# A fused attention and two-mixture kernel: key buffer by expert, half of one expert's low parts on GpSimd, a new order

## The chip, the cores and the metric

The kernel runs on one core of one Trainium2 chip. The metric is the device time of one execution in microseconds (us). Three runs of the kernel before took 522.6, 523.45 and 535.63 us; their median, 523.45 us, is the time before.

## The reference, cut to what matters

Three stages follow one another, each on 4 batches of 576 tokens of width 512.

1. Windowed attention with 8 heads of 64: four heads see the last 32 positions, four see every fourth of the last 128.
2. A mixture of 4 attention experts. Each expert `e` has its own `q = x @ wq[e]`, `k = x @ wk[e]`, `v = x @ wv[e]` of width 64, a causal softmax over all 576 positions, and an output projection `wo[e]`. Each token adds up its two best experts with softmax weights.
3. A mixture of 8 feed-forward experts (512 to 1024 to 512, with a relu). One expert per token: its own best, or that of the token before it where a local gate says so. The result is scaled by a softmax probability.

## The kernel before, in words

Products are made in float16 with split operands: a value becomes a high part (`hi`, rounded) and a low part (`lo`, what rounding lost), and a product is the sum of high by high, high by low and low by high. The helper `split` (line 476 on) makes both parts: ScalarE (ACT) writes `hi` as a scaled copy, VectorE (DVE) writes `lo` with one scalar-tensor-tensor instruction. For a kind of split that `KN` lists, ACT writes a second, float32 scaled copy `f32t` (three buffers), and GpSimd (POOL) subtracts `hi` from it. Before the change only the kind "x2" goes that way.

Stages 1 and 2 and the first three blocks of stage 3 ("early slots", `eslot`, line 1358 on) form one part. Its instructions are recorded first, each with an estimated cost, its dependencies and a unit number; `Plan.order` (line 284 on) then schedules them in a list and issues them on five in-order queues: TensorE (PE), DVE, ACT, POOL and SyncE (SP), which starts the DMAs. The unit offsets `OFF` are the priorities: among the instructions that could start first on an engine, the unit with the lower offset goes first. There are 263 units (a projection half, an attention unit, a tile of the output projection, and so on).

Dependencies in the planner come from `region` and `hits`: an operand is a range of partitions and a range of bytes, from its first to its last. Two operands with the same two-row stride can be told apart inside those ranges; an operand of one run and one of two rows can't. Outside the planner, the framework that places the semaphores finds its own dependencies between the instructions.

For each batch `proj` (line 740 on) multiplies the tokens with the query and key weights in four groups `m` (queries of experts 0 and 1, keys of 0 and 1, queries of 2 and 3, keys of 2 and 3). Each group is split into a buffer `qkhl`, and DMAs carry it to the places where the attention reads it: four small ones per query group into `qs`, four per key group into `kk`, one for each expert and half of the partitions. `kk` holds, for each partition, four experts by high and low part by 576 positions. It has two buffers in turn: that of batches 0 and 2 lies in the large tile `share` (its DMAs read `share<-qkhl` in the trace), that of batches 1 and 3 is a tile of its own (`kk<-qkhl`). An attention unit (`at_a`, line 830 on) takes one tile of queries and one, two or four experts, and multiplies with the high and the low part of each expert's keys.

After the last batch's attention and routing come 19 slots (`slot`, line 1334 on) in a fixed order, each with the two products of one block of 128 tokens, while the next slot's weights are loaded and split. That part is not planned and not changed.

`w_split` (line 1266 on) splits the first expert's weights for the early slots: eight chunks of 128x1024, each in two halves of 512 columns, 16 splits of kind "w". In the slots after them both parts are made over whole chunks on ACT and DVE directly.

Of the kernel before, what the change touches and what calls it, by code (L numbers as in the profile page):

```python
# [11 lines left out]
F16 = mybir.dt.float16  # L12
I32 = mybir.dt.int32
AF = mybir.ActivationFunctionType
OP = mybir.AluOpType
# [9 lines left out]
E1 = 4  # L25
# [3 lines left out]
STATIC = 21  # L29
NEG = -float(2.0 ** 60)  # L30
XW = DM + 1
OFF = (-5462.82, 15301.63, 15749.23, 2741.58, 15715.62, 23895.09, 23839.59, -4159.48, -20321.99, 19270.96, 3973.86,
# [26 lines left out]
KN = {"x0": (0, 1), "qk": (0, 1), "v2": (0, 1), "x2": (1, 1), "yt": (0, 1), "w": (0, 1), "f32t": 3,  # L59
      "early": 3, "pfl": (100000,), "wn": 224, "xp": "XA", "warm": 80, "off": OFF,  # L60
      "xgb": 3, "x2b": 3, "hx": "X", "hy": "A", "h2": "X", "fc": (0, 4),
      "banks": {"S": 2, "T": 2, "A": 2, "X": 1, "Y": 1}, "share": 32740, "emax": 23840,
# [376 lines left out]
def tile_attention_moe_moe(ctx: ExitStack, tc, qd, kd, vw, wqk, wvg, wo, woT, wg9, w1, w2,  # L439
# [36 lines left out]
    def split(src, hi, lo, scale, kind=None):  # L476
        c = CNT[kind] = CNT.get(kind, -1) + 1
        num, den = KN.get(kind, (0, 1))
        A.activation(hi, src, AF.Copy, scale=float(scale))
        if c % den >= num:  # L480
            V.scalar_tensor_tensor(lo, src, float(scale), hi, op0=OP.mult, op1=OP.subtract)
            return
        if not isinstance(src, View):
            P.scalar_tensor_tensor(lo, src, float(scale), hi, op0=OP.mult, op1=OP.subtract)
            return
        n = int(np.prod(hi.shape[1:]))
        f = sm.tile([128, 512], F32, name="f32t", bufs=KN["f32t"])
        r = src.shape[0]
        f = f[:r, :n] if len(hi.shape) < 3 else f[:r, :n].rearrange("p (a b) -> p a b", a=hi.shape[1])
        A.activation(f, src, AF.Copy, scale=float(scale))  # L490
        P.tensor_tensor(lo, f, hi, op=OP.subtract)
# [248 lines left out]
    def proj(b):  # L740
        xh, xl = XH[b], XL[b]
        qs = pr.tile([128, E1, S], F16, name="qs2")
        kk = pr.tile([128, 2, E1, S], F16, name="kk2")
        vh = pr.tile([128, NT, E1, 65], F16, name="vh2")
        vl = pr.tile([128, NT, E1, 65], F16, name="vl2")
        QK[b] = (qs, kk, vh, vl)
        for m in (0, 2, 1, 3):
            q = pr.tile([128, 2, S], F16, name="qkhl")
            for i in range(2):
                c = slice(288 * i, 288 * i + 288)  # L750
                o = ps("A", [128, 288])
                for d in range(4):
                    w = wh[:, d, m * 128:m * 128 + 128]
                    T.matmul(o, w, xh[:, d, c], start=(d == 0), stop=False)
                    T.matmul(o, w, xl[:, d, c], start=False, stop=False)
                    w = wl[:, d, m * 128:m * 128 + 128]
                    T.matmul(o, w, xh[:, d, c], start=False, stop=(d == 3))
                split(o, q[:, 0, c], q[:, 1, c], 2.0 ** -9, "qk")
                yield 1.45
            for par in range(2):  # L760
                r = slice(64 * par, 64 * par + 64)
                e = 2 * (m % 2) + par
                for z in range(2):
                    zr = slice(64 * z, 64 * z + 64)
                    if m < 2:
                        SQ.dma_start(qs[zr, e, :], q[r, z, :])
                    else:
                        SQ.dma_start(kk[zr, :, e, :], q[r, :, :])
        if b < 2:
            P.memset(vh[:, :, :, 64:65], 512.0)  # L770
            P.memset(vl[:, :, :, 64:65], 0.0)
# [58 lines left out]
    def at_a(u):  # L830
        b, t, es = UNITS[u]
        qs, kk, _, _ = QK[b]
        s = sm.tile([128, S], F32, name="s2")
        mx = tiny.tile([128, 4], F32, name="mx2")
        if t < 4:
            ext = 128 * t + 128
            p = ps("S", [128, len(es), ext])
            for z, e in enumerate(es):
                w = qs[:, e, 128 * t:128 * t + 128]
                T.matmul(p[:, z, :], w, kk[:, 0, e, :ext], start=True, stop=False)  # L840
                T.matmul(p[:, z, :], w, kk[:, 1, e, :ext], start=False, stop=True)
            for z, e in enumerate(es):
                V.tensor_tensor_reduce(out=s[:, ext * z:ext * z + ext], in0=p[:, z, :],
                                       in1=tri[:, 512 - 128 * t:640],
                                       scale=-esc, scalar=3.0e38, op0=OP.add, op1=OP.min,
                                       accum_out=mx[:, z:z + 1])
            for z, e in enumerate(es):
                c = slice(ext * z, ext * z + ext)
                A.activation(s[:, c], s[:, c], AF.Exp, scale=-1.0, bias=mx[:, z:z + 1])
        else:  # L850
            for z in range(2):
                p = ps("S", [128, 288])
                c = slice(288 * z, 288 * z + 288)
                for h, e in enumerate(es):
                    w = qs[:, e, 512:576]
                    o = p[64 * h:64 * h + 64, :]
                    T.matmul(o, w, kk[:, 0, e, c], start=True, stop=False)
                    T.matmul(o, w, kk[:, 1, e, c], start=False, stop=True)
                V.tensor_tensor_reduce(out=s[:, c], in0=p, in1=tri2 if z else tri[:, 0:288],
                                       scale=-esc, scalar=3.0e38, op0=OP.add, op1=OP.min,  # L860
                                       accum_out=mx[:, z:z + 1])
            V.tensor_tensor(mx[:, 2:3], mx[:, 0:1], mx[:, 1:2], op=OP.min)
            A.activation(s, s, AF.Exp, scale=-1.0, bias=mx[:, 2:3])
        UA[u] = s
# [660 lines left out]
```

## Time and profile before

| what | us |
|---|---|
| median of the runs shown | 523.45 |
| the runs | 522.6, 523.45, 535.63 |
| the profiled execution | 531.6 |
| its span, first to last instruction | 529.6 |
| around the span | 2.0 |
| planned part, to the first matmul of the 19 slots | 310.2 |
| 19 slots and the end | 219.4 |

Read it as two parts. In the planned part PE, DVE and ACT share the work in an order that the planner chose; in the 19 slots PE works without a pause. The clock that the chip grants TensorE is one of two levels, 2.4 and 1.2 GHz; the profile writes them as 1.00 and 0.50, and its mean over the span is 0.964.

### The profile page before, as it was taken

The numbers are of one execution on the slowest core, as the hardware profiler recorded it, in microseconds if no ns is written. First come the engines' busy times: TensorE is split into PE (matmuls) and PEld (weight loads), VectorE is DVE, ScalarE is ACT, GpSimd is POOL, SyncE is SP. The second block draws the span as 40 slices with busy tenths as digits, with TensorE's granted clock in tenths as the row PEclk, the third lists the DMA queues.
The fourth block names the chain that finished last, engine by engine and source line by source line (L and its number), as shares of the span: only waits on it lengthen the run. The fifth ranks groups of instructions, "written<-read, shape, count | busy, mean of one in ns | idle before, by whom it ended". The sixth has DMA issues, their size and how long they took to land.

```text
span 529.6 us, 17318 instructions
## 1 busy us (share of the span) xinstructions
PE 499.1 (94%) x6802; PEld 384.5 (73%) x6802; DVE 423.3 (80%) x1225; ACT 370.3 (70%) x624; POOL 136.4 (26%) x165
## 2 busy tenths in 40 slices
PE   7799789999999999999799999999999999999992
PEld 6688678888887787776566776777767776677760
DVE  4855467788669879899897249999999999999993
ACT  4353344565666757687484159999999999999992
POOL 7845315341000001132200212132111321123211
PEclk9959978999999999999889999999999999999997
DMA  9773866332422321122571753774146199461110
GB/s 317 308 242 110 262 195 223 114 109 59 98 55 47 76 48 43 44 81 71 175 295 33 238 200 117 274 256 155 45 168 231 35 336 399 167 226 58 61 45 15
DMA packets 32727, 79.90 MB, mean 151 GB/s; under 512 B 7166, under 2 KB 15870, under 8 KB 31616
## 3 DMA queue, kind: packets, MB, share of 16 engines
q1 hardware_dynamic: 28960, 67.71, 37.8%
q0 software_dynamic: 3680, 11.03, 6.1%
q8 instruction: 55, 0.90, 0.7%
q14 instruction: 32, 0.26, 0.2%
HBM read 112.52 MB, written 10.49 MB: 232 GB/s over the span
## 4 chain that ended last, share of the span: by engine, by line
PE 40%; issue 23%; DMA 22%; DVE 9%; ACT 2%; POOL 1%; POOLq 0%; SPq 0%; DVEq 0%; ACTq 0%
DMA out_dram<-o,SIDX 17%; PE A L416 17%; PE S L416 6%; PE T L416 6%; PE X L416 6%; PE Y L416 4%; DVE s L416 2%; DVE tl L416 2%; DMA share<-in_vw_dram 2%; DMA share<-x2d,GIDX 1%; DMA share<-qkhl 1%; DVE share L416 1%; DVE r L416 1%; ACT share L1273 1%; DVE OHV L416 1%
## 5 line engine op out<-in xcount | busy, mean ns | idle before, releaser
L1274 DVE SCALAR_TENSOR_TENSOR share<-share 128x1024 f16<-128x1024 f32 x152 | 177.4, 1219 | 16.5 <-ACT share L1273 16.5
L1273 ACT ACTIVATE share<-share 128x1024 f16<-128x1024 f32 x152 | 149.9, 1048 | 0.6 <-DMA share<-in_w_dram 0.5
L416 PEld LDWEIGHTS <-share 128*128 128x128 f16 (+1 forms) x1438 | 112.4, 101 | 45.4 <-issue 7.3
L1308 PE MATMUL S<-share 128*128 128x128 f16 x608 | 102.8, 219 | 0.0
L1307 PE MATMUL S<-share 128*128 128x128 f16 x608 | 102.8, 219 | 0.0
L1309 PE MATMUL S<-share 128*128 128x128 f16 x608 | 102.8, 219 | 0.0
L416 PE MATMUL A<-share 128*128 128x288 f16 (+3 forms) x816 | 88.9, 267 | 3.9 <-DVE qkhl L416 3.7
L1328 POOL DMA_INDIRECT out_dram<-o,SIDX x19 | 27.0, 1418 | 155.0 <-ACT o L1325 146.9
L1308 PEld LDWEIGHTS <-share 128*128 128x128 f16 x608 | 59.5, 98 | 2.3
L1307 PEld LDWEIGHTS <-share 128*128 128x128 f16 x608 | 59.5, 98 | 2.3
L1309 PEld LDWEIGHTS <-share 128*128 128x128 f16 x608 | 59.5, 98 | 0.0
L1319 PE MATMUL A<-share 128*128 128x512 f16 x152 | 57.7, 380 | 0.0
L1321 PE MATMUL A<-share 128*128 128x512 f16 x152 | 57.4, 378 | 0.0
L1320 PE MATMUL A<-share 128*128 128x512 f16 x152 | 57.4, 378 | 0.0
L416 ACT ACTIVATE th<-T 128x512 f16<-128x512 f32 (+3 forms) x84 | 42.1, 513 | 21.3 <-PE T L416 20.1
L416 ACT ACTIVATE s<-s,mx 128x512 f32<-128x512 f32 (+4 forms) x72 | 40.7, 582 | 14.6 <-DVE mx L416 13.2
L416 ACT ACTIVATE share<-A 128x288 f16<-128x288 f32 (+3 forms) x67 | 30.0, 447 | 27.2 <-PE A L416 22.0
L416 POOL TENSOR_TENSOR share<-f32t,share 128x512 f16<-128x512 f32 (+1 forms) x15 | 16.0, 1067 | 117.8 <-ACT f32t L416 71.9
L416 DVE CUSTOM_DVE_ANT_0 s<-S,tri 128x256 f32<-128x256 f32 (+4 forms) x80 | 37.1, 476 | 9.1 <-PE S L416 8.7
L416 PE MATMUL S<-share 128*64 128x64 f32 (+5 forms) x672 | 38.7, 252 | 2.0 <-DMA share<-qkhl 2.0
L416 DVE SCALAR_TENSOR_TENSOR tl<-T,th 128x512 f16<-128x512 f32 (+2 forms) x60 | 35.6, 595 | 1.0 <-ACT th L416 0.8
L416 PE MATMUL T<-ident,s 128*128 128x128 f32 (+1 forms) x200 | 33.1, 285 | 0.8 <-ACT s L416 0.7
(207 smaller groups left out, 940.2 us busy)
## 6 DMA issues: line engine op xcount, KB each, us to landing
share<-in_w_dram SPq DMA_DIRECT2D x160, 512.0 KB
share<-in_vw_dram SPq DMA_DIRECT2D x8, 1152.0 KB
share<-in_kd_dram SPq DMA_DIRECT2D x8, 608.0 KB
share<-in_qd_dram SPq DMA_DIRECT2D x8, 576.0 KB
x2d<-share SPq DMA_DIRECT2D x16, 256.0 KB
share<-qkhl SPq DMA_DIRECT2D x16, 144.0 KB
kk<-qkhl SPq DMA_DIRECT2D x16, 144.0 KB
share<-share SPq DMA_DIRECT2D x16, 72.0 KB
```

The source lines that it names most:

```text
L416: getattr(q, name)(*[bind(x) for x in a], **{n: bind(x) for n, x in k.items()})
L1273: A.activation(h, stg[:, c, :], AF.Copy, scale=64.0)
L1274: V.scalar_tensor_tensor(l, stg[:, c, :], 64.0, h, op0=OP.mult, op1=OP.subtract)
L1307: T.matmul(p[:, i, :], wh_[:, c], xt[:, d, :], start=(d == 0), stop=False)
L1308: T.matmul(p[:, i, :], wh_[:, c], xt[:, 4 + d, :], start=False, stop=False)
L1309: T.matmul(p[:, i, :], wl_[:, c], xt[:, d, :], start=False, stop=(d == 3))
L1319: T.matmul(p, hh[:, f, :], wh_[:, a], start=(f == 0), stop=False)
L1320: T.matmul(p, hh[:, f, :], wl_[:, a], start=False, stop=False)
L1321: T.matmul(p, hl[:, f, :], wh_[:, a], start=False, stop=(f == 7))
L1328: return nc.gpsimd.indirect_dma_start(out=orows, out_offset=bass.IndirectOffsetOnAxis(ap=SIDX[:, t:t + 1], axis=0), in_=o, in_offset=None, ...
```

## The change

Three things. The key buffer becomes four experts by two parts by 576 positions, instead of two parts by four experts by 576, so that one expert's high and low rows lie next to each other, and each DMA fills one run per partition. The kind "w" gets the setting (1, 2): every second half-chunk split of the first expert's weights takes the `f32t` and POOL way. And all unit offsets are new numbers. A branch of `split` in which POOL would read a source from SBUF directly, and which no kind reached before, is gone.

```diff
 OFF = (...264 numbers, all replaced...)
-KN = {"x0": (0, 1), "qk": (0, 1), "v2": (0, 1), "x2": (1, 1), "yt": (0, 1), "w": (0, 1), "f32t": 3,
+KN = {"x0": (0, 1), "qk": (0, 1), "v2": (0, 1), "x2": (1, 1), "yt": (0, 1), "w": (1, 2), "f32t": 3,
@@ split
         if c % den >= num:
             V.scalar_tensor_tensor(lo, src, float(scale), hi, op0=OP.mult, op1=OP.subtract)
             return
-        if not isinstance(src, View):
-            P.scalar_tensor_tensor(lo, src, float(scale), hi, op0=OP.mult, op1=OP.subtract)
-            return
@@ proj
-        kk = pr.tile([128, 2, E1, S], F16, name="kk2")
+        kk = pr.tile([128, E1, 2, S], F16, name="kk2")
@@
-                        SQ.dma_start(kk[zr, :, e, :], q[r, :, :])
+                        SQ.dma_start(kk[zr, e], q[r, :, :])
@@ at_a
-                T.matmul(p[:, z, :], w, kk[:, 0, e, :ext], start=True, stop=False)
-                T.matmul(p[:, z, :], w, kk[:, 1, e, :ext], start=False, stop=True)
+                T.matmul(p[:, z, :], w, kk[:, e, 0, :ext], start=True, stop=False)
+                T.matmul(p[:, z, :], w, kk[:, e, 1, :ext], start=False, stop=True)
@@
-                    T.matmul(o, w, kk[:, 0, e, c], start=True, stop=False)
-                    T.matmul(o, w, kk[:, 1, e, c], start=False, stop=True)
+                    T.matmul(o, w, kk[:, e, 0, c], start=True, stop=False)
+                    T.matmul(o, w, kk[:, e, 1, c], start=False, stop=True)
```

## Rows read from the trace of the kernel before

**Rows 1.** The page's first part: busy time, share of the span, instructions.

```profile
PE 499.1 (94%) x6802; PEld 384.5 (73%) x6802; DVE 423.3 (80%) x1225; ACT 370.3 (70%) x624; POOL 136.4 (26%) x165
```

**Rows 2.** Busy time by stretch: start:end, length, each engine's busy us, granted clock, DMA share.

```profile
26.00:42.00 16.00, 15.42 (x286) 12.82 (x286) 7.96 (x39) 7.04 (x17) 8.98 (x18) 0.57 0.70 243
...
70.00:80.00 10.00, 8.50 (x131) 7.86 (x131) 6.02 (x32) 4.42 (x12) 2.28 (x2) 0.66 0.75 244
80.00:86.00 6.00, 6.00 (x146) 5.48 (x146) 4.37 (x37) 2.96 (x6) 4.32 (x3) 0.72 0.70 255
86.00:250.00 164.00, 162.33 (x2427) 129.22 (x2425) 134.73 (x571) 108.68 (x253) 31.55 (x23) 1.00 0.27 76
250.00:266.00 16.00, 11.81 (x155) 9.51 (x151) 12.88 (x72) 6.99 (x15) 4.30 (x4) 0.89 0.53 179
266.00:282.00 16.00, 16.00 (x155) 10.27 (x155) 15.95 (x38) 12.64 (x24) 0.00 (x0) 0.89 0.56 214
...
310.00:520.00 210.00, 209.34 (x2434) 154.34 (x2432) 197.87 (x190) 197.82 (x229) 48.22 (x38) 1.00 0.47 165
```

**Rows 3.** Timeline of PE and ACT: start, length, instruction, idle time before and releaser.

```profile
56.87 0.42 ACT L416 ACTIVATE share<-share 128x264 f16<-128x264 f32 x1 [2.51 <-DMA share<-in_wvg_dram]
...
60.06 0.88 PE L416 MATMUL A<-share 128*64 128x132 f16 x24 [3.73 <-DVE qkhl L416]
...
69.21 0.27 PE L416 MATMUL S<-share 128*128 128x256 f16 x1
71.50 1.28 PE L416 MATMUL S<-share 128*128 128x256 f16 x11 [2.02 <-DMA share<-qkhl]
```

**Rows 4.** The same timeline for SP's queue, around the key DMAs.

```profile
48.96 5.44 SPq L416 DMA_DIRECT2D share<-qkhl  x4
54.49 0.54 SPq L416 DMA_DIRECT2D share<-in_wvg_dram  x1
...
61.14 8.27 SPq L416 DMA_DIRECT2D share<-qkhl  x4
...
121.00 2.59 SPq L416 DMA_DIRECT2D kk<-qkhl  x4
```

**Rows 5.** Waits of SP's queue: for what, us in total, times, longest.

```profile
SPq L416 <- DMA share<-qkhl: 9.6, 6, 2.8
...
SPq L416 <- DMA share<-in_vw_dram: 2.4, 1, 2.4
```

**Rows 6.** Stretches of 2 us around the two pauses, columns as in rows 2.

```profile
58.00:60.00 2.00, 0.00 (x0) 0.00 (x0) 0.45 (x2) 1.23 (x3) 0.00 (x0) 1.00 1.03 373
...
70.00:72.00 2.00, 0.50 (x6) 0.48 (x7) 0.26 (x1) 0.17 (x1) 0.00 (x0) 0.99 0.85 216
72.00:74.00 2.00, 2.00 (x56) 1.80 (x57) 1.61 (x12) 1.35 (x4) 0.00 (x0) 0.50 1.04 401
```

**Rows 7.** Issues of the key and query DMAs: shortest, median, longest in ns.

```profile
L416 SPq DMA_DIRECT2D qs<-share x16: 462/575/1567, 95.8 to 218.6; - x16
...
L416 SPq DMA_DIRECT2D kk<-qkhl x16: 591/608/697, 121.0 to 192.0; - x16
```

**Rows 8.** Groups by shape: two of 263 to 283 us, two of the span.

```profile
L416 DVE SCALAR_TENSOR_TENSOR share<-share 128x512 f16<-128x512 f32 x16 | 10.4, 672 | 0.2 <-issue 0.2
L416 ACT ACTIVATE share<-share 128x512 f16<-128x512 f32 x16 | 9.0, 623 | 0.0
...
L416 POOL TENSOR_TENSOR share<-f32t,share 128x512 f16<-128x512 f32 x12 | 14.0, 1166 | 110.4 <-ACT f32t L416 64.7 <-PE A L416 31.5 <-ACT th L416 6.7
L416 ACT ACTIVATE f32t<-A 128x512 f32<-128x512 f32 x12 | 7.1, 591 | 0.0
```

**Rows 9.** Timeline of POOL and DVE where they overlap.

```profile
30.72 0.82 POOL L416 TENSOR_TENSOR share<-share,r 128x378 f32<-128x378 f32 x1 [0.94 <-DVE r L416]
31.33 0.75 DVE L416 SCALAR_TENSOR_TENSOR share<-share 128x512 f16<-128x512 f32 x1 [0.39 <-ACT share L416]
31.50 1.27 POOL L416 TENSOR_TENSOR share<-share,mx 128x378 f32<-128x378 f32 x1
```

More of the change, by code (lines that the diff above doesn't have):

```diff
@@ L31 @@
 XW = DM + 1
-OFF = (-5462.82, 15301.63, 15749.23, 2741.58, 15715.62, 23895.09, 23839.59, -4159.48, -20321.99, 19270.96, 3973.86,
[26 rows of a table removed]
-KN = {"x0": (0, 1), "qk": (0, 1), "v2": (0, 1), "x2": (1, 1), "yt": (0, 1), "w": (0, 1), "f32t": 3,
+OFF = (15079.06, -14073.05, -6228.6, -13230.76, -11311.75, -9136.75, -14304.07, 29513.66, -6714.41, -9107.27,
[26 rows of a table added]
+KN = {"x0": (0, 1), "qk": (0, 1), "v2": (0, 1), "x2": (1, 1), "yt": (0, 1), "w": (1, 2), "f32t": 3,
       "early": 3, "pfl": (100000,), "wn": 224, "xp": "XA", "warm": 80, "off": OFF,
```

52 rows, old and new, of the table OFF are left out of this document.

## The prediction, made before the change was run

> **What bounds the kernel now.** I read the page's busy shares first, then busy time by stretch, then the waits of the stretches with pauses. PE is busy 94% of the span [rows 1], so a saving is a pause of PE that closes or a stretch in which its clock rises again. By stretch [rows 2] most of the span has neither: from 86 to 250 us PE is busy 162.33 of 164 us, and in the slots, 310 to 520, 209.34 of 210, all at the full clock. The change doesn't touch the slots. What is left stands in three places. From 26 to 42 us the clock is at 0.57: (1 - 0.57) x 16 = 6.9 us are lost there. From 56 to 86 us PE pauses twice, for 3.73 and 2.02 us [rows 3], and the clock then falls: 0.66 over 10 us and 0.72 over 6 us lose 3.4 + 1.7 = 5.1 us [rows 2]. From 250 to 266 us PE idles 16 - 11.81 = 4.2 us, and the clock's 0.89 there and in the next 16 us loses 2 x 1.8 = 3.5 us.
>
> Both pauses of the second place lead back to the key DMAs. In SP's queue the four for batch 0's first key group take 5.44 us and those for the second 8.27 us, against 2.59 us for four of batch 1, whose buffer is a tile of its own [rows 4]. The difference is waiting: SP waited six times, 9.6 us in all, for an earlier `share<-qkhl` [rows 5]. Nothing in the data asks for that, since the four fill different places. But a two-row write of one expert spans, from its first byte to its last, the rows of the others, and a wait of up to 2.8 us between such writes is what a dependency on overlapping ranges looks like. What stands behind it in SP's queue pays: the load of a slice of `wvg` is issued at 54.49 us, right after the four [rows 4]; ACT, in order, sits 2.51 us until it lands, the eviction of `qkhl` behind it is late, and PE pauses 3.73 us for it [rows 3]. The second group's last DMA is late in the same way, and PE, one matmul into its first attention unit, pauses 2.02 us for it [rows 3].
>
> **The change part by part.** *Key layout.* Each write becomes one run per partition, disjoint from every other, so the waits between them should go, in the planner's dependencies too: a unit of experts 0 and 1 no longer needs the keys of 2 and 3. First term: the 2.8 us that SP is held before the `wvg` load [rows 5]. Of PE's 3.73 us this can return 0 (another load is the late one) to 3.7; I take the 2.51 us that ACT waited for exactly that load, 2.5. Next late would be the `wo` and `vw` loads in the same stretch. Second term: PE's pause for the second group, 0 to 2.0 us; I take 2.0, since units of experts 0 and 1 can fill it even if the DMAs stay late (SP's 2.4 us for `in_vw` [rows 5] is a load's and may stay). Third term: the clock. It was at 1.00 after PE had done nothing from 58 to 60 us, and at 0.50 from 72 us on, after a stretch in which PE was busy 0.50 of 2 us [rows 6]. If the pauses go, 0 to 5.1 us come back; the first pause left the clock up, the second didn't, so I take half, 2.5. The number of DMAs stays at 32, at 0.608 us each to issue; one run instead of two rows might bring them to the 0.575 us of a query write [rows 7], 32 x 0.033 = 1.1 us of SP, which has gaps: nothing.
>
> *Low parts on POOL.* Eight of the 16 half-chunks leave DVE: 8 x 10.4 / 16 = 5.2 us less there. ACT gets eight more copies, at 7.1 / 12 = 0.59 us [rows 8]: 4.7 us more. POOL gets 8 x 1.17 = 9.3 us and does nothing from 266 to 282 us [rows 2]. PE is busy 16.00 of 16 us in that stretch, so less DVE work there returns nothing at once: 0. The cover is PE's own backlog of output projection and early slots. If it is gone, ACT is the one to fear: 12.64 + 4.7 = 17.3 us of work in 16, 1.3 us too much. Everything behind those copies on ACT (evictions that free PSUM for PE) would wait as long. At best relieving DVE shortens the pauses just before, which belong to the last attention units, not to the weights; I bound the term at a gain of 1 and a loss of 4.1 us (the loss below) and take 0, since nothing in the rows shows PE short of work there.
>
> A POOL subtraction of 0.82 us took 1.27 us at 31.50 us, while DVE ran a split with two SBUF inputs [rows 9]: the two engines took turns. If that holds for the weights, eight POOL subtractions and the eight DVE splits left need 9.3 + 5.2 = 14.5 us in turn, where 16 splits on DVE needed 10.4: 4.1 us later, and only just inside the 16 us of the stretch. The Trainium skill, "SBUF — State Buffer", section "Who interferes with whom", has this as a rule: a DVE instruction with two SBUF inputs contends with a GpSimd instruction that reads SBUF, and whoever comes first keeps the port for the whole instruction. By the rule the sum would lose up to 4.1 us, by a POOL that is simply idle nothing; the trace agrees with the rule in the row at 31.50 us.
>
> *New order.* Every unit of the planned part moves, every queue is passed, and no instruction is added. From 86 to 250 us PE has 1.7 us of pauses to give [rows 2], so nothing there can gain. The gain is bounded by the third place, 4.2 + 3.5 = 7.7 us; the loss by a new low-clock stretch (below), 10.6. Neither is in the rows, so I take 0, between the two and nearest to 86 to 250 us, most of the part.
>
> *Sum.* 2.5 + 2.0 + 2.5 + 0 + 0 = 7.0 us, between 0 and 10.8 for the layout alone. Against the profiled execution, 531.6 us: 524.6. That one was 8.15 us above the median; none of my terms uses the stretch from 26 to 42 us, whose 6.9 us are the likeliest cause, so I take the 7.0 from the median: 523.45 - 7.0 = 516.5 us.
>
> **The rivals.** *The order pays too.* The layout's 7.0 us, and the new offsets put output projection into the pauses from 250 to 266 us: 6.5 of the 7.7 us. 510 us. For it: 4.2 us of pause with DVE busy 12.88 of 16 us [rows 2], and the low parts' move relieves DVE right behind. Against it: those units are the end of a chain that must run in sequence.
>
> *The port.* POOL and DVE take turns and the low parts come 4.1 us later: 516.5 + 4.1 = 520.6 us. For it [rows 9]; against it, the second product of the first early slot is what needs the last ones, and other PE work can go ahead.
>
> *The pauses only change their name.* DMA engines are busy all of 58 to 60 us, 1.03 [rows 6]; if the loads are what is late, PE waits for them instead, and the time stays at 523.5 us.
>
> *Slower: attention too early.* Units of experts 0 and 1 may now start around 56 us, in the place of projections. They are chains of PE, DVE, ACT and PE, with little PE work each; if PE becomes as thin as from 70 to 72 us [rows 6], the clock stays low for a stretch like 26 to 42 us, 6.9 us, with a pause like the 3.73 us: 10.6 more, 534 us. It decides once a pause like that of 70 to 72 us turns up early in the part with a 0.50 behind it.
>
> **How the numbers follow.** Chances: the forecast 0.40 (its own range 512 to 521 us), the order pays too 0.30, the port 0.10, the pauses stay 0.12, slower 0.08. The range 507 to 524 us leaves out the slower rival, and some of the order's best and the layout's worst, under 0.2 together. Two per cent, about what a measurement of this kernel can tell from no change, are 10.5 us: faster below 513.0, slower above 533.9. Faster: 0.8 of the order's 0.30 and 0.15 of the forecast's 0.40, 0.30. Slower: most of the last rival, 0.07. Within: 0.63.
>
> **What would show it.** SP's waits for `share<-qkhl` gone, and the four key DMAs of batches 0 and 2 in some 2.6 us as in batch 1; the first attention matmuls before the second key group has landed; no pause of PE over 1 us between 56 and 72 us, and the clock at 1.00 from 70 to 86; POOL subtractions of 1.17 us or more in the weights' stretch, DVE below 15.95 there; the first of the 19 slots some 7 us earlier, and their length unchanged. I am wrong if SP still waits between key writes, if loads hold PE from 56 to 60 us, or if the clock falls in a place where it was at 1.00.

## The result, and the profile after

The changed kernel took 520.04 us (median of 11 runs, 518.06 to 522.0), the kernel before, on the same chip, 525.84 us (11 runs, 522.6 to 535.63). The ratio is 0.9872, 95% interval [0.9839, 0.9905]: some 1.3% faster, within the 2%. On another chip a second set of runs gave 518.52 us and 0.984 [0.9763, 0.9916]. The forecast was 516.5 / 523.45 = 0.9867. Ratios and intervals leave out a kernel's runs that are over 1.5% above its fastest.

The profiled execution took 520.04 us, its span 518.2. The first slot's first matmul comes at 298.7 us (310.2 before), and slots and end last 219.5 us (219.4 before), so the 11.5 us between the two profiles lie wholly in the planned part. That pair shows more than the medians, since the execution profiled before was one of its longer ones. The page's first part, for [rows 1]:

```profile
PE 490.8 (95%) x6802; PEld 377.2 (73%) x6802; DVE 423.6 (82%) x1217; ACT 373.1 (72%) x632; POOL 145.8 (28%) x173
```

Eight instructions left DVE, and eight each came to ACT and POOL, as the weights' setting asks. Busy time by stretch of the changed kernel, for [rows 2] (start:end, length, busy us of PE, weight load, DVE, ACT, POOL, granted clock, DMA share, GB/s):

```profile
26.00:42.00 16.00, 13.25 (x249) 10.42 (x249) 9.14 (x48) 7.29 (x18) 10.22 (x19) 0.89 0.72 251
42.00:56.00 14.00, 13.40 (x288) 11.27 (x287) 10.53 (x59) 8.03 (x20) 8.92 (x15) 1.00 0.82 265
56.00:60.00 4.00, 4.00 (x87) 3.37 (x83) 3.06 (x28) 1.16 (x4) 0.63 (x1) 1.00 0.62 155
60.00:70.00 10.00, 9.19 (x198) 8.21 (x197) 7.71 (x35) 7.27 (x20) 5.73 (x4) 1.00 0.80 241
70.00:80.00 10.00, 10.00 (x169) 8.25 (x170) 8.22 (x53) 5.22 (x12) 5.45 (x4) 1.00 0.84 298
80.00:86.00 6.00, 6.00 (x106) 5.61 (x105) 4.63 (x26) 3.20 (x10) 4.32 (x3) 1.00 0.42 96
86.00:250.00 164.00, 159.46 (x2380) 125.91 (x2379) 137.28 (x590) 108.43 (x252) 25.55 (x21) 1.00 0.26 74
250.00:266.00 16.00, 13.11 (x133) 9.41 (x132) 10.20 (x24) 11.64 (x25) 8.45 (x8) 0.81 0.70 270
266.00:282.00 16.00, 16.00 (x216) 11.87 (x214) 14.16 (x54) 8.25 (x15) 4.32 (x4) 1.00 0.20 61
282.00:310.00 28.00, 28.00 (x299) 19.38 (x297) 11.88 (x16) 13.68 (x18) 5.43 (x5) 1.00 0.56 198
```

From 56 to 86 us PE idles 0.8 us of 30 at the full clock; before, its two pauses of 3.73 and 2.02 us and a clock of 0.66 and 0.72 stood there [rows 2, 3]. That place alone is worth some 10 us. From 26 to 42 us the clock is at 0.89 instead of 0.57, 5.1 us, while PE idles 2.2 us more: 3 us that no term of the prediction has. From 86 to 250 us PE idles 164 - 159.46 = 4.5 us, 2.8 more than before. From 250 to 266 us it idles 2.9 us instead of 4.2, and the clock is at 0.81 there instead of 0.89, and at 1.00 instead of 0.89 in the 16 us after it.

SP's queue and PE of the changed kernel by time, for [rows 4]:

```profile
43.34 3.51 SPq L416 DMA_DIRECT2D share<-qkhl  x4
48.06 0.38 SPq L416 DMA_DIRECT2D share<-in_wvg_dram  x1
54.44 1.75 SPq L416 DMA_DIRECT2D share<-qkhl  x3
60.09 0.51 SPq L416 DMA_DIRECT2D share<-qkhl  x1
```

```profile
49.87 0.60 PE L416 MATMUL S<-share 128*128 128x256 f16 x4
```

The first key group takes 3.51 us instead of 5.44. The second is sent in two pieces of 1.75 and 0.51 us, between 54.44 and 60.60 us, with other DMAs between them, where before it took 8.27 us in one go. The four matmuls at 49.87 us are attention of experts 0 and 1: they start before the second key group is sent at 54.44 us, as the disjoint ranges allow. What SP and PE waited for (us in all, times, longest; the first row is SP's only wait that has to do with `qkhl`, the other three are all of PE's between 26 and 75 us):

```profile
SPq L416 <- DVE qkhl L416: 16.0, 5, 4.9
```

```profile
PE S L416 <- POOL share L416: 1.9, 4, 0.8
PE T L416 <- POOL share L416: 1.6, 1, 1.6
PE X L416 <- DVE share L416: 0.3, 1, 0.3
```

SP's six waits for an earlier `share<-qkhl`, 9.6 us, and that for `in_vw` [rows 5] are gone. What is left is a wait for data: DVE has still to make the keys' low part. Before, that wait was 6.6 us, so in all SP waits as long for the keys as it did (16.0 against 9.6 + 6.6 us), but no longer for another key write.

### The profile page after: what moved, and what is told of

It is laid out like the page before. It is cut to its first block, busy times and chain, and to the rows that moved or that the text cites. A ratio compares the mean times of both kernels' runs of the same rounds, so it can differ in the third digit from the quotient of the medians.

```text
span 518.2 us, 17329 instructions
## 1 busy us (share of the span) xinstructions
PE 490.8 (95%) x6802; PEld 377.2 (73%) x6802; DVE 423.6 (82%) x1217; ACT 373.1 (72%) x632; POOL 145.8 (28%) x173
## 4 chain that ended last, share of the span: by engine, by line
PE 35%; issue 24%; DMA 23%; DVE 10%; POOL 3%; ACT 2%; POOLq 0%; SPq 0%; DVEq 0%; ACTq 0%
DMA out_dram<-o,SIDX 18%; PE A L416 17%; PE T L416 5%; PE S L416 5%; PE Y L416 4%; PE X L416 4%; DVE share L416 3%; POOL share L416 3%; DMA out_dram<-share,SIDX 2%; DMA share<-in_wo_dram 2%; DVE tl L416 1%; DVE s L416 1%; DVE r L416 1%; ACT share L416 1%; DMA share<-in_qd_dram 1%
## 5 line engine op out<-in xcount | busy, mean ns | idle before, releaser
L416 PE MATMUL A<-share 128*128 128x288 f16 (+3 forms) x816 | 87.6, 266 | 0.4 <-ACT L L416 0.2
L416 POOL TENSOR_TENSOR share<-f32t,share 128x512 f16<-128x512 f32 (+1 forms) x23 | 25.9, 1130 | 104.9 <-ACT f32t L416 92.3
L416 ACT ACTIVATE s<-s,mx 128x512 f32<-128x512 f32 (+4 forms) x72 | 40.5, 582 | 13.2 <-DVE mx L416 11.5
L416 PE MATMUL S<-share 128*64 128x64 f32 (+4 forms) x672 | 36.5, 236 | 2.5 <-POOL share L416 1.9
L416 DVE SCALAR_TENSOR_TENSOR share<-A,share 128x288 f16<-128x288 f32 (+3 forms) x52 | 24.2, 465 | 11.9 <-ACT share L416 11.6
```

Source lines behind the costliest of these rows:

```text
L416: getattr(q, name)(*[bind(x) for x in a], **{n: bind(x) for n, x in k.items()})
```

## The experiments

All kernels by what they contain; "old*" and "new*" mean that the planner was told the addresses of the other layout, so that every engine's order is that of the kernel which the row is compared with. Ratios are against the kernel before on the same chip.

| kernel | key layout | low parts on POOL | offsets | extra matmuls | ratio, 95% interval |
|---|---|---|---|---|---|
| changed kernel | new | half | new | no | 0.9872 [0.9839, 0.9905] |
| changed kernel, again | new | half | new | no | 0.984 [0.9763, 0.9916] |
| layout alone, order kept | new* | none | old | no | 0.9996 [0.994, 1.0052] |
| layout alone, planned anew | new | none | old | no | 0.9913 [0.985, 0.9976] |
| changed, old layout | old* | half | new | no | 0.9947 [0.9892, 1.0003] |
| changed, low parts on DVE | new | none | new | no | 0.9925 [0.9873, 0.9978] |
| low parts alone | old | half | old | no | 1.0058 [1.0022, 1.0094] |
| offsets alone | old | none | new | no | 1.0348 [1.0281, 1.0416] |
| changed, old offsets | new | half | old | no | 1.0017 [0.9966, 1.0068] |
| before, filled | old | none | old | 64 | 1.0012 [0.997, 1.0054] |
| layout alone, filled | new* | none | old | 64 | 0.9897 [0.9832, 0.9962] |
| changed, old layout, filled | old* | half | new | 64 | 0.9985 [0.9946, 1.0024] |
| changed, filled | new | half | new | 64 | 0.9887 [0.9825, 0.9949] |

**The layout alone, in before's order.** The instructions of every engine and their order are those of the kernel before; only the shape of the key DMAs and the addresses differ. The two lines that matter of the edit (the reads in `at_a` change too, and a function tells the planner the old addresses):

```diff
-        kk = pr.tile([128, 2, E1, S], F16, name="kk2")
+        kk = pr.tile([128, E1, 2, S], F16, name="kk2")
...
-                        SQ.dma_start(kk[zr, :, e, :], q[r, :, :])
+                        SQ.dma_start(kk[zr, e], q[r, :, :])
```

> The kernel before with the new key layout alone; every engine's instructions stay in the order of the kernel before. The waits theory (SP was held 9.6 us by waits between key writes, and that made the two pauses of PE at 56 and 69.5 us): SP's waits for share<-qkhl at 0, the pause of 3.73 us down to about 1.2, that of 2.02 us gone, 4 to 7 us less, a ratio of 0.987 to 0.992. The order theory (the gain comes from the new offsets): the waits may go, but loads end the pauses, ratio 0.998 to 1.002.

Measured: 0.9996 [0.994, 1.0052], the medians 528.42 and 530.2 us. The profile says more than that. Its stretches:

```profile
56.00:60.00 4.00, 3.34 (x65) 3.03 (x64) 3.04 (x17) 1.52 (x6) 2.34 (x3) 1.00 1.00 349
60.00:70.00 10.00, 9.06 (x193) 7.65 (x193) 6.66 (x47) 5.53 (x17) 1.62 (x2) 1.00 0.94 280
70.00:80.00 10.00, 9.53 (x183) 8.84 (x179) 8.13 (x56) 5.13 (x13) 6.60 (x5) 0.83 0.74 236
80.00:86.00 6.00, 5.96 (x85) 4.83 (x84) 5.10 (x28) 2.87 (x10) 3.32 (x2) 1.00 0.72 219
```

By time, its SP queue, ACT behind the `wvg` load, and PE:

```profile
48.79 2.38 SPq L416 DMA_DIRECT2D share<-qkhl  x4
57.91 4.96 SPq L416 DMA_DIRECT2D share<-qkhl  x4
...
54.72 0.42 ACT L416 ACTIVATE share<-share 128x264 f16<-128x264 f32 x1 [0.53 <-DMA share<-in_wvg_dram]
56.83 0.88 PE L416 MATMUL A<-share 128*64 128x132 f16 x24 [0.66 <-DVE qkhl L416]
66.39 0.38 PE L416 MATMUL S<-share 128*128 128x256 f16 x2 [0.24 <-DMA share<-qkhl]
67.46 0.82 PE L416 MATMUL S<-share 128*128 128x256 f16 x10 [0.70 <-DMA share<-in_kd_dram]
71.62 1.85 PE L416 MATMUL A<-wg,share 128*128 128x9 f32 x16
```

ACT's wait for the `wvg` load fell from 2.51 to 0.53 us, PE's pause behind it from 3.73 to 0.66, and the second from 2.02 to 0.24, with 0.70 us for another load behind it. From 56 to 86 us this leaves 2.1 us idle and 10 x 0.17 = 1.7 us of clock, 3.8 in all, where before had 5.75 + 5.1 = 10.85: 7.0 us back. The matmul on `wg`, which reads only what comes before, moved from 78.83 us to 71.62, and the slots start at 304.0 instead of 310.2. The second key group still takes 4.96 us, 2.5 of them SP's wait for the `in_vw` load. So the mechanism is there, and is worth 6 to 7 us in one pair of profiles, while the runs show nothing. The pair flatters it: the execution profiled here, 525.52 us, is the lowest of its six, that of before one of the longer. In the first set of runs that was the riddle.

**The layout alone, planned anew.** Here the planner sees the new layout's dependencies, with the old offsets and no low parts on POOL.

> The kernel before with the new key layout, and the planner sees it, so that it may start units of experts 0 and 1 earlier; offsets and the weights' low parts as before. The waits theory: as the run with the order kept, 4 to 7 us less, 0.987 to 0.992, and another 1 us at most from units that start earlier. The order theory: a plan with offsets that were not made for these dependencies is no better than before, 0.998 to 1.01.

Measured: 0.9913 [0.985, 0.9976]. But the order is hardly another one: by operation, shape and tile, 8 of 1225 places in DVE's order, 4 of 624 in ACT's and 16 of 6802 in PE's hold another instruction than before, and none in POOL's and SP's. So this is nearly the same program as the one above, and yet the counted runs of the two, on one chip, differ by 4.4 +- 2.7 us. Taken together they are 2.2 +- 2.8 us faster than before: from these two alone the layout's worth is not clear of zero, and the riddle is one of the runs, not of the order.

**The changed kernel with the old layout.** The reverse of the first: the changed kernel's order of every engine, with keys by part and then by expert.

> The changed kernel, every engine in its order, with the key buffer laid out as before. The waits theory: SP waits for share<-qkhl again, some 9 us in all; what stands behind the key writes comes late, and the gain of 6.7 us is mostly lost: ratio to the kernel before 0.995 to 1.003. The order theory: the new order keeps its gain, 0.986 to 0.990.

Measured: 0.9947 [0.9892, 1.0003]. The waits of SP and then of PE (before the slots) in this kernel:

```profile
SPq L416 <- DMA share<-qkhl: 9.3, 5, 3.9
```

```profile
PE T L416 <- DVE y L416: 4.0, 1, 4.0
...
PE S L416 <- DMA share<-qkhl: 3.3, 2, 2.0
```

The old layout brings the waits back: 9.3 us in SP's queue and 3.3 us of PE. In this order 0.8 to 1.1% of the gain (0.9947 against 0.9872 and 0.984, measured on other chips, with overlapping intervals) hangs on the layout.

**The changed kernel with all low parts on DVE.**

```diff
-KN = {... "w": (1, 2), ...
+KN = {... "w": (0, 1), ...
```

> The changed kernel with all low parts of the first expert's weights on VectorE again; layout and offsets as changed. The port theory (a POOL subtraction held a VectorE instruction of the last attention chain for 1.2 us at 253 us, and PE waited 2.64 us for that chain): 0.5 to 2 us faster than the changed kernel, ratio to the kernel before 0.983 to 0.986. The relief theory (moving low parts to POOL is part of the gain): 1 to 4 us slower than the changed kernel, 0.989 to 0.995.

Measured: 0.9925 [0.9873, 0.9978], 524.41 us. Its last stretches ahead of the slots:

```profile
266.00:282.00 16.00, 15.02 (x199) 10.81 (x198) 12.45 (x52) 4.53 (x8) 0.00 (x0) 1.00 0.25 70
282.00:310.00 28.00, 25.89 (x305) 19.17 (x303) 7.20 (x9) 9.26 (x14) 6.46 (x6) 1.00 0.55 193
```

PE idles 1.0 and 2.1 us where in the changed kernel it idles 0.0 and 0.0, and the slots start at 303.0 us instead of 298.7. Late low parts are not the reason: DVE makes the last of the 16 at 267.28 us, while in the changed kernel POOL's last one starts at 269.22. The longest of the pauses stands in front of the second product of an early slot, for the low part of its hidden layer:

```profile
297.82 5.35 PE L416 MATMUL X<-share 128*128 128x512 f16 x24 [1.75 <-DVE share L416]
```

There PE has nothing else left to do. Where the difference begins can be told: up to one copy of ACT the two kernels run ACT's instructions in the same order, and reach it at the same time. The first row is this kernel, the second the changed one.

```profile
249.07 0.38 ACT L416 ACTIVATE yth<-T 128x256 f16<-128x256 f32 x1 [1.63 <-PE T L416]
```

```profile
249.11 0.38 ACT L416 ACTIVATE yth<-T 128x256 f16<-128x256 f32 x1 [1.54 <-PE T L416]
```

From there to the slots it is 303.0 - 249.1 = 53.9 us here and 298.7 - 249.1 = 49.6 in the changed kernel, and 49.6 again in its second profile. The same way takes 48.5 us in the kernel before and 48.7 with the layout alone. So with the new offsets the low parts on POOL are worth 4.3 us of the profile, all behind 249 us; they take back what these offsets cost at the end. Behind that point the planner's order differs, and DVE has 13.00 us of work from 250 to 266 us instead of 10.20; how much is order and how much is that work isn't separated. In the runs all low parts on DVE cost some 0.5 to 0.9% against the changed kernel, measured on other chips, with overlapping intervals.

**The changed kernel again**, to carry it to another chip with the three that follow.

> The changed kernel, unchanged, on one chip with the three runs that follow, so that they can be set against it. All theories: 0.985 to 0.990.

Measured: 0.984 [0.9763, 0.9916], 518.52 us, the slots again from 298.6 us.

**The low parts alone.** Before, with the setting (1, 2) for "w".

> The kernel before with only the low parts moved: every second half-chunk of the first expert's weights on GpSimd, offsets and key layout as before. The port theory: nothing gained, up to 2 us lost, 0.999 to 1.004. The relief theory: 1 to 4 us gained, 0.992 to 0.998.

Measured: 1.0058 [1.0022, 1.0094]: a small loss, so the relief theory fails; the medians of all runs, 530.69 and 529.59 us, lie closer together. Its stretches and PE's longest wait:

```profile
26.00:42.00 16.00, 14.55 (x402) 12.23 (x395) 10.35 (x44) 9.48 (x23) 10.89 (x23) 1.00 0.77 256
...
56.00:60.00 4.00, 3.72 (x53) 3.34 (x53) 2.29 (x10) 0.73 (x4) 2.68 (x2) 0.50 0.97 301
```

```profile
PE A L416 <- DVE qkhl L416: 4.5, 1, 4.5
```

PE's instructions up to 42 us stand in the same order as before, yet the clock there is 1.00 and not 0.57 [rows 2]. The slots start at 309.3 us, hardly sooner than before's 310.2: in the profile the gain is gone again by 60 us, in a wait of 4.5 us for the same chain from the key DMAs over the `wvg` load to `qkhl`, which is there as before, and in the low clock behind it. From the copy `yth<-T` of the section above to the slots it takes 52.6 us, 4.1 more than before.

**The offsets alone.** Before, with the new `OFF`.

> The kernel before with only the new offsets; key layout and weights as before. The early-clock theory (what the new order gives is that PE is not thin from 20 to 26 us, so the clock does not fall for the 16 us after it, 6.9 us): a granted clock over 0.85 in 26 to 42 us, 3 to 7 us gained, 0.986 to 0.994. The layout theory (the order gives nothing without the new layout): 0.998 to 1.01.

Measured: 1.0348 [1.0281, 1.0416], 3.5% slower. Two stretches:

```profile
86.00:250.00 164.00, 152.12 (x2250) 120.78 (x2248) 125.84 (x532) 100.63 (x236) 22.83 (x18) 0.99 0.23 63
...
266.00:282.00 16.00, 12.68 (x103) 8.86 (x101) 13.61 (x40) 11.83 (x25) 3.26 (x3) 0.57 0.76 301
```

PE idles 11.9 us from 86 to 250, where it idles 1.7 with the old offsets [rows 2] and 4.5 in the changed kernel; then 3.3 us more and a clock of 0.57 from 266 to 282. The early-clock theory had its condition (0.89 from 26 to 42 us) and not its gain. The changed kernel with low parts on DVE differs from this one in the layout alone, and took 0.9925; and an order planned with the new layout but run on the old one still took 0.9947 (there with low parts on POOL). So what spoils the long middle is the order that the planner makes of these offsets with the old layout's dependencies.

**The changed kernel with the old offsets.**

> The changed kernel with the offsets of before: new key layout and moved low parts, old order of priorities. The early-clock theory: a granted clock of 0.50 to 0.60 in 26 to 42 us as before, and 0 to 4 us gained, 0.992 to 1.000. The layout theory: the gain stays, 0.985 to 0.990.

Measured: 1.0017 [0.9966, 1.0068], with a clock of 0.89 from 26 to 42 us: the layout theory fails, and the early-clock theory had the time about right and the clock wrong. Set against the changed kernel on the same chip, the old offsets cost 9.0 +- 3.0 us. With all low parts on DVE they cost nothing: the freely planned layout, with old offsets, and the changed kernel with low parts on DVE, on one chip, differ by 0.7 +- 2.6 us, the new offsets being the slower. So offsets and low parts belong together, and that is clear of noise. How it splits is less so: under old offsets the low parts cost (1.0058 alone; 0.9913 to 1.0017 with the layout, on two chips, with intervals that just overlap); under the new they pay in the profile (4.3 us, above). From the copy `yth<-T` to the slots this kernel takes 50.9 us, 2.2 more than the layout alone. In this kernel low parts of both engines stand close together, and rows of PE, POOL and DVE show what that costs:

```profile
267.62 0.23 PE L416 MATMUL X<-share 128*128 128x128 f16 x1 [1.03 <-POOL share L416]
...
272.12 1.09 POOL L416 TENSOR_TENSOR share<-f32t,share 128x512 f16<-128x512 f32 x1 [0.83 <-ACT f32t L416]
...
272.59 1.16 DVE L416 SCALAR_TENSOR_TENSOR share<-share 128x512 f16<-128x512 f32 x1 [0.15 <-ACT share L416]
```

The DVE split takes 1.16 us and not 0.67 [rows 8]; four of the eight took 1.07 us or more, in the changed kernel one. And PE, in the first product of an early slot, waits 1.03 us for a part that POOL makes; with the low parts alone it waits the same 1.03 us, at 270.90. Neither before nor the changed kernel has that wait.

**Four kernels with PE kept busy early.** What differed between runs of one kernel was the mean clock: on the chip of the first set, the spans of before ran from 523.1 us (clock 0.981 to 0.990) to 530.6 (0.972 or less), while all six of the layout alone had 0.965 to 0.976. The early stretch, at 0.57 in the profiles of both and at 1.00 in others, was the suspect. 64 matmuls whose result nobody reads were added behind the warm-up, the same in all four kernels:

```diff
+        for j, i in enumerate(seq):
+            if j > last and self.ops[i].eng == "T" and n < FILLS:   # FILLS = 8, last: the last warm-up
+                n += 1
+                for _ in range(8):
+                    self.fill()   # Y[:, :224] <- zero x zero
```

> The kernel before with 64 extra matmuls (8 of 224 columns each, into the bank of the warm-up, whose result nobody reads, ahead of each of the first 8 TensorE operations after the last warm-up) so that TensorE does not pause between 19.6 and 26 us. Theory 'the clock lottery hides the layout': the stretch 26 to 42 us, at 0.57 in the profile of before and at 1.00 in that of the kernel with only the weights' parameter, runs at 1.00 in every run; the extra work is 64 x 0.093 = 6 us at full clock, of which some 3.4 us fill pauses, so 1.00 to 1.005 against before, with a narrower spread of the runs. Rival 'the stretch is not what makes the runs differ': the spread of before stays and the low clock comes back somewhere between 26 and 60 us.

> The new key layout alone in before's order of every engine, with the same 64 extra matmuls at the same places as the filled kernel before. Theory 'the pauses are worth their length once the early clock is the same': 4 to 7 us under the filled kernel before (ratio to it 0.987 to 0.993), since the pause at 56 us and that at 69.5 us go and the stretch 70 to 80 us runs at a higher clock. Rival 'given back later': the same time as the filled kernel before within 1.5 us; then the stretches after 86 us, above all 250 to 282 us, must be longer by what the pauses gave.

> The changed kernel's order and weights' parameter with the old key layout, with the 64 extra matmuls. Theory 'the layout is worth its waits in either order': slower than the filled changed kernel by the same 4 to 7 us as the filled kernel before is than the filled layout alone. Rival 'the layout pays only in the order made for it': 4 to 6 us here, and nothing in before's order. Second rival 'order and layout are one thing': here the same time as the filled kernel before.

> The changed kernel with the 64 extra matmuls. Theory 'the clock lottery is a part of the change's gain' : against the filled kernel before the gain shrinks to under 1% (ratio above 0.99), since before's unlucky early clock is gone. Rival 'the gain is in the order and the waits': the ratio of filled changed to filled before stays at 0.984 to 0.987, as without the extra matmuls.

Measured, medians: 530.27, 524.22, 528.91 and 523.59 us. The stretch from 26 to 42 us of the filled kernel before, which is at 1.00 in the profiles of the other three too, and a later one:

```profile
26.00:42.00 16.00, 14.64 (x336) 12.70 (x329) 9.61 (x41) 8.24 (x20) 8.71 (x18) 1.00 0.68 238
...
70.00:80.00 10.00, 10.00 (x222) 9.41 (x222) 7.29 (x43) 5.87 (x16) 3.66 (x3) 0.67 0.67 220
```

The narrower spread that I expected did not come: the filled kernel before ran from 526.11 to 537.37 us, the unfilled one on that chip from 524.85 to 534.34. So the early stretch is not what makes the runs differ, or not alone; the low clock stands at 70 us in that profile, and what makes the runs differ stays open. How many runs had the early stretch at the full clock isn't recorded.

With these four on one chip, the layout is worth the same in both orders. Means of the runs counted, 95% intervals of their differences by a t-test: 529.9 to 525.0, 4.9 +- 2.7 us, in before's order; 528.8 to 523.6, 5.2 +- 1.1 us, in the new one. In the new order the profiles show it too, 527.1 and 521.3 us of span. With the old layout these waits of SP and PE (before the slots) are there; with the new one neither is:

```profile
SPq L426 <- DMA share<-qkhl: 7.9, 4, 4.3
```

```profile
PE S L426 <- DMA share<-qkhl: 2.6, 2, 2.1
```

New order and low parts together give 1.2 +- 1.5 us with the old layout and 1.4 +- 2.6 with the new, neither clear of zero. So "given back later" falls in this set, and so does "only in the order made for it". That the early clock makes up much of the change's gain falls too: the theory asked for a ratio above 0.99 and it is 523.6 / 529.9 = 0.988; filled, the change is worth 6.4 +- 1.6 us, against some 6.7 and 8.4 unfilled by the ratios, so that a small part isn't excluded.

One profile can mislead here. The execution of the filled layout that was profiled took 529.04 us, the slowest of its six, and has this row, a pause of PE that nothing recorded explains:

```profile
73.46 0.27 PE L426 MATMUL T<-ident,s 128*128 128x128 f32 x1 [2.62 <-issue]
```

Its slots start at 307.4 us, those of the filled kernel before at 307.6, so in before's order the filled profiles don't show the gain that the runs show. Whether the other five had that pause isn't known; they took 522.8 to 526.9 us.

## Why the prediction was right, point by point

**The layout's 7.0 us** is what held. The steps were shown one by one: SP no longer waits between key writes, the `wvg` load comes sooner, ACT's wait for it and PE's pause behind it go (first term 2.5, measured 3.73 - 0.66 = 3.1), the pause for the second key group goes (second term 2.0, measured 2.02 - 0.94 = 1.1, since a load, `in_kd`, is the next late), and the clock rises from 70 to 86 us (third term 2.5, measured 5.1 - 1.7 = 3.4). The four writes did not all shrink to the 2.6 us that I named as a sign (2.38 and 4.96 us in the layout alone). The sum in the profile of the layout alone is 7.0 with the remaining idle time; over runs it is 4.9 and 5.2 us in the filled kernels, and 2.2 +- 2.8 us unfilled. Sized a little high, and right in kind. That the whole change came so close to the sum, 0.9872 to 0.9867, is in part luck: some 5 us of layout and some 1.3 us, not clear of zero, of two terms that I had put at nothing.

**Taking it from the median** was right. The early low-clock stretch comes and goes in kernels of one order (0.57 in before, 1.00 with the low parts alone), and no term used it. The median itself was that of three runs; with eleven it is 525.84, and 2.4 of the 3.5 us between 516.5 and 520.04 come from there. That the stretch is the likeliest cause of the 8.15 us above the median isn't shown: the filled kernel before spreads as much. What I didn't see is that the spread of the runs can also hide a change: the layout alone, unfilled, measured 0.2 +- 2.7 us. At a like clock (before's four counted runs at 0.976 or less have a mean span of 529.4 us, the six of the layout alone 526.5) it was 2.9 us shorter. The mean clock is in part an outcome, so that comparison is a hint only, and why all six fell low stays open.

**Low parts, 0**: failed as a price of its own. I bounded it by how full DVE, ACT and POOL would be from 266 to 282 us, between a gain of 1 and a loss of 4.1 us. With old offsets it cost 0.6% (3 us) alone and 1.0% (5 us) beside the layout; with the offsets made for it, it returned 0.5 to 0.9% (3 to 5 us, intervals overlapping). The profiles put both behind the copy `yth<-T`: 4.1 and 2.2 us lost with old offsets, 4.3 gained with the new, pauses and clock together, and the gain not through earlier low parts, as their early end on DVE shows. The step that failed is that nothing leaves PE short of work there: from 266 to 310 us it idles 3.1 us with all low parts on DVE and not at all in the changed kernel. Which instruction the gain begins with stays open. The cover that I named, PE's backlog, wasn't complete either: with old offsets PE waits 1.03 us for POOL in front of an early slot, about a third or less of the loss, while the changed kernel has no such wait.

**New order, 0**: again right for the sum (1.2 and 1.4 us, neither clear of zero) and wrong in kind. I bounded the loss by a low-clock stretch of 10.6 us; alone the offsets lose 3.5%, through 10 more us of pauses between 86 and 250 us, where I had said that nothing could gain and had not asked what could be lost, and through the clock behind it. They aren't a third gain beside the other two: with the low parts on POOL they are worth 9.0 +- 3.0 us against the old offsets, without them nothing.

**The rivals.** *The order pays too* (510 us) did not come: PE's idle time from 250 to 266 us fell by 1.3 us, the clock there fell as well, and the middle lost 2.8. *The pauses only change their name* fell with the row of 56 to 60 us. *Attention too early* had its start right (49.87 us) and its end wrong: PE is not thin there, and the clock from 42 to 86 us is 1.00. *The port* was half right. Its 520.6 us is near the measured 520.04 by the lower median alone; as a ratio it is 0.9946, outside the interval. POOL and DVE do take turns, as in the rows of 272 us above, and small instructions pay as well; the rows are POOL, DVE and PE of the changed kernel, then the same pair of DVE instructions and the same matmul with all low parts on DVE:

```profile
252.08 2.14 POOL L416 TENSOR_TENSOR share<-f32t,share 128x512 f16<-128x512 f32 x2
...
253.08 1.33 DVE L416 SCALAR_TENSOR_TENSOR r<-r,gw 64x2 f32<-64x2 f32 x2
...
254.93 0.66 PE L416 MATMUL T<-twin,y 128*128 128x64 f32 x4 [2.64 <-DVE y L416]
```

```profile
253.54 0.32 DVE L416 SCALAR_TENSOR_TENSOR r<-r,gw 64x2 f32<-64x2 f32 x2
...
254.97 0.66 PE L416 MATMUL T<-twin,y 128*128 128x64 f32 x4 [2.56 <-DVE y L416]
```

Two instructions of 64x2 took 1.33 us instead of 0.32 beside POOL's subtraction. The Trainium skill, "SBUF — State Buffer", section "Who interferes with whom", says that a DVE instruction with two SBUF inputs contends with a GpSimd instruction that reads SBUF, and these rows agree. But PE gained nothing where POOL was out of the way: it waits 2.56 us for that chain instead of 2.64, since two DVE splits of 0.68 us, at 252.73 and 253.89 us, now run between its instructions. So the 4.1 us of that rival did not reach the end of the changed kernel: POOL's low parts are spread over 252 to 271 us there, PE waits for none of them directly, and without them the profile is longer. With the old offsets a wait of PE for POOL shows, at 1.03 us.

## What to carry to other kernels

A large buffer written in pieces should be laid out so that each piece is one run: ranges that only interleave can be taken for overlapping, and the queue that waits for them makes everything behind it late, loads that have nothing to do with it above all. Priorities that were searched for belong to the dependencies and costs they were searched with; priced alone, such a change of order looks like a loss, and so does the part that it was made for. Where a kernel's runs differ by more than the effect, a few runs of two nearly equal programs can lie 4 us apart: keep the order of every engine, take both kernels on one chip with more runs, and ask the traces where the difference begins, before saying that an effect is not there.

## What the hardware showed that was not expected

The granted clock of one stretch differed between kernels whose instructions up to its end stand in one order: 0.57 from 26 to 42 us in the kernel before, 1.00 with only the low parts moved, 0.89 in the changed kernel with the old offsets. Filling the pauses ahead of that stretch bought nothing that the runs show: the filled kernel before took 530.27 us against 531.31 for before (means 0.4 +- 1.8 us the other way). Its extra matmuls follow each other at 0.096 us, 64 x 0.096 = 6.1 us, of which 11.48 - 8.39 = 3.1 us lie in pauses between 14 and 26 us, so some 3 of the possible 6.9 us were spent outside them; in how many runs of before that stretch is at the low clock isn't recorded.

The DVE instructions that paid for POOL's subtractions were not only large ones: a pair of 64x2 took four times its 0.32 us.
